# Clustered attention and two mixture layers on one core: a tile for each PSUM bank, weights converted in halves

## The chip, the cores and the metric

The kernel runs on one core of a Trainium2 chip. The metric is the device time of one execution in microseconds (us). The engines are PE (TensorE, matrix multiplies and transposes), ACT (ScalarE), DVE (VectorE), POOL (GpSimd) and SP (SyncE, which here issues nearly all DMAs). Each engine works through its own list of instructions in order and waits on semaphores.

## The reference, cut to what matters

```python
q_assign = argmax(q_n . c_n);  k_assign = argmax(k_n . c_n)      # 16 clusters per head
mask = q_assign[:, :, :, None] == k_assign[:, :, None, :]
scores = where(mask, scale * q @ k.T, -1e9);  attn = softmax(scores)
x = (attn @ v) as 1536 tokens x 512                               # B, H, S, D = 2, 8, 768, 64
h = x @ w_in  (512 x 2048);  x = (h * cos(h)) @ w_out             # first mixture
h = x @ w2_in;  g = h if h >= 1, 0 if h <= -1, else (h + 1)**2 / 4
out = g @ w2_out                                                  # second mixture
```

The weights arrive as 64-bit floating point numbers, two 32-bit words each, and are put together on the chip.

## The kernel before

**Attention** goes through the sixteen heads as eight pairs. A cycle of the program treats one pair and prepares the one two cycles on. What is emitted in a cycle is written out in a string of words (`CYCLE`, with `BEGIN` for the first cycle, `LATE` and `LAST` for the seventh and eighth, and `END` behind them). A quote behind a word means the pair of the cycle before. `S` is a tile of scores (128 rows by 768, four matmuls, L583 and L586) and its row maximum on DVE (L593); `E` its exponential on ACT (L601); `G` three PE transposes of probabilities into one PSUM bank (L644) and their copy to SBUF on ACT (L646); `V` the product with `v` (L651), which adds up in the fourth bank; `T` the other head's transpose on DVE (L677) and `W` its product (L686), which uses all four banks; `X` and `Y` scale and split the first head's result (L656, L663 to L667); `Z` and `z` do so for the second (L696, L697, L705 to L707); `R` and `B` invert the row sums and spread them by DMA. `Q`, `D`, `C`, `m`, `t`, `n`, `O`, `H`, `J`, `L` prepare a pair to come: transposes of q and k (L491), cluster products (L510), their transpose (L518), the first largest (L527 to L538), its transpose (L545, L547), stacking by DMA (`copy`, L473) and loading. `w` is one step of weight conversion.

PSUM has eight banks. Four are held by a single tile, `big`, of four banks; `bank3` hands out its first three in turn to all transposes and cluster products. The scores have two tiles of two banks each. The recording layer that sets the semaphores takes `big` as one thing.

**Weights.** A weight of 512 x 512 comes as two chunks of 128 x 1024 (`issue_chunk`, one raw buffer `wraw`, 1 MB a load), and is converted in six steps (`convert_chunk`): a magnitude on ACT (L157), four integer and clipping steps on DVE (L159 to L167), the high part on POOL (L173), the low part on DVE (L176). Twelve steps, one weight, are done in the last two cycles, the rest between the matmuls of the mixtures.

**Mixtures.** For each of 4 columns of weights and 3 blocks of 512 tokens, `hidden` makes four tiles `h` of 12 matmuls (three products of high and low parts, L859 to L861) in four PSUM banks, and applies the function with ACT and DVE (`g_cosine`: L832 to L838; `g_blend`: L847 to L852), POOL (L821) and DVE (L825) splitting the result. `output` makes four tiles `y` of the block before and adds them up (L905, L914).

What sets the order: `manual_schedule` keeps the order in which the code emits for the attention. It is closed ahead of the mixtures, whose order a scheduler chooses from priorities; it also puts pieces of them among the attention's last instructions.

Of the kernel before, what the change touches and what calls it, by code (L numbers as in the profile page):

```python
# [19 lines left out]
P = 128  # L20
# [6 lines left out]
CHUNK = 6  # L27
P_BUFS = 8
# [5 lines left out]
def attention_moe_moe(  # L34
# [104 lines left out]
    def shared(name):  # L139
        return w0pool.tile([P, 2, 512], F32, tag="wx", bufs=1, name=name)  # L140

    def issue_chunk(n):
        if n >= len(wchunks):
            return
        src, c0, _ = wchunks[n]
        raw = w0pool.tile([P, 2, 512], I64, tag="wraw", bufs=1, name=f"wraw{n}")
        nc.sync.dma_start(raw, src[:, c0:c0 + 2])
        wraw[n] = raw

    def convert_chunk(n):  # L150
# [8 lines left out]
        nc.vector.tensor_scalar(x, x, HIGH_MIN, HIGH_MAX, ALU.max, ALU.min)  # L159
# [12 lines left out]
        hi, lo = t[:, 0, c0:c0 + 2], t[:, 1, c0:c0 + 2]  # L172
        nc.gpsimd.tensor_scalar(hi, x, 1.0, 0.0, ALU.mult, ALU.add)  # L173
        issue_chunk(n + 1)
        yield
        nc.vector.tensor_tensor(lo, x, hi.bitcast(F32), ALU.subtract)  # L176
        yield

    for l, (wi, wo) in enumerate(((w1_in, w1_out), (w2_in, w2_out))):
        for qi in range(NQ):  # L180
            cols = slice(qi * 512, (qi + 1) * 512)
            for s, src in enumerate((wi[:, cols], wo[cols])):
                for c0 in (0, 2):
                    wchunks.append((src.rearrange("(c p) f -> p c f", p=P), c0,
                                    (l * NQ + qi) * 2 + s))
# [16 lines left out]
    def weight(l, qi, s):  # L202
        pump(2 * CHUNK * ((l * NQ + qi) * 2 + s + 1) - at[0])
        t = wslot[((l * NQ + qi) * 2 + s) % len(wslot)]
        return t[:, 0], t[:, 1]


    with ExitStack() as actx:
# [17 lines left out]
        def load_qk(i):  # L226
# [38 lines left out]
        def centroid_setup(ct):  # L265
# [6 lines left out]
            nat[1] = w0pool.tile([P, 2, NJ, 2, D], F32, tag="wraw", bufs=1, name="nat1")  # L272
            nc.scalar.activation(nat[1][:, :, 0, 0, 0:1].rearrange("p s o -> p (s o)"),
# [17 lines left out]
        def first_pair():  # L291

            idle_o = big[:, 3]
# [16 lines left out]
            both = shared("both0")  # L310
            dots = [both[:, 0, :HS].rearrange("p (j s h c) -> p j s h c", s=2, h=2, c=C),
# [64 lines left out]
            dc = both[:, 1, :HS].rearrange("p (j n) -> p j n", n=P)  # L376
# [16 lines left out]
            eqs = both[:, 1, :HS].rearrange("p (h g c) -> p h g c", h=2, c=C)  # L393
# [81 lines left out]
        class Prep:  # L475
# [26 lines left out]
            def dots(self):  # L502
                both = shared(f"both{self.i}")
                self.ohv, self.eq = both[:, 0, :HS], both[:, 1, :HS]
# [144 lines left out]
        def p_v(i, kt):  # L649
            for hf in range(2):  # L650
                nc.tensor.matmul(big[hf * D:(hf + 1) * D, 3, :HS], v_of[i][:, kt],  # L651
                                 pts.pop((i, 2 * kt + hf)), start=kt == 0, stop=kt == NJ - 1)

        def x_rows(i):
            x = rb[2 * i]
            nc.vector.tensor_tensor(x, big[:, 3, :HS], x, ALU.mult)  # L656
# [22 lines left out]
        def p_v_square(i, n, parts):  # L679
            t, vr = sq[i], vr_of[i]  # L680
            for cp in range(12 * n // parts, 12 * (n + 1) // parts):
                for a in range(4):
                    rows = slice(32 * a, 32 * a + 32)
                    for par in range(2):
                        kt, g = divmod(2 * cp + par, 4)
                        nc.tensor.matmul(  # L686
                            big[par * D:(par + 1) * D, a, :NJ * 32],
# [31 lines left out]
        def run_cycle(c, order):  # L719
# [4 lines left out]
            for word in words:  # L724
# [8 lines left out]
                if not 0 <= i < NP and what != "w":  # L733
                    if what == "L" and i == NP:
                        issue_chunk(0)
                    continue
# [50 lines left out]
                elif what == "w":  # L787
                    pump(arg or 1)

        BEGIN = ("L' S3 m' E3 S4 t' S5 E4 H0' n' G0 E5 R0 O' G1 G2 S6 G3 G4 J0' E6 S7 G5 r T6 V0 E7 H1' V1 G6 "  # L790
                 "G7 S8 T7 B0 Q0 J1' E8 G8 G9 Q1 V2 S9 T8 G10 G11 Q2 Q3 L S10 E9 E10 T9 V3 D S11 E11 C m V4 t "
                 "n ")
# [3 lines left out]
        LATE = ("S0 S1 H0' E0 E1 T10' O' V5' S2 S3 E2 w E3 J0' T11' X' G0 S4 E4 w v' S5 W0' W1' R1' J1' E5 R0 "  # L796
                 "w W2' W3' Y' Z' S6 S7 G1 B1' G2 G3 E6 G4 E7 V0 H1' V1 w T6 T7 G5 G6 G7 S8 G8 r G9 G10 E8 w "
                 "S9 B0 T8 V2 E9 V3 S10 G11 w S11 E10 T9 E11 z' V4 ")
        LAST = ("S0 S1 E0 E1 w T10' V5' S2 S3 E2 E3 T11' X' G0 S4 E4 w v' S5 W0' W1' R1' E5 R0 w W2' W3' Y' "
                 "Z' S6 S7 G1 B1' G2 G3 E6 G4 E7 V0 V1 w T6 T7 G5 G6 G7 S8 G8 r G9 G10 E8 w S9 B0 T8 V2 E9 V3 "  # L800
                 "S10 G11 w S11 E10 T9 E11 z' V4 ")
        END = ("T10' V5' T11' X' R1' W0' B1' W1' W2' W3' Z' Y' z' ")
# [4 lines left out]
        manual.close()  # L807
# [55 lines left out]
    def hidden(l, qi, blk):  # L863
# [4 lines left out]
        for f in range(4):  # L868
# [7 lines left out]
            pump(2 if l == qi == blk == 0 else 1)  # L876
        return gh, gl

    def output(l, qi, blk, gh, gl):
        wh, wl = weight(l, qi, 1)  # L880
        for e in range(4):
# [18 lines left out]
            pump(2 if l == qi == 0 else 1)  # L900
# [64 lines left out]
```

## Time and profile before

| | |
|---|---|
| median of three runs | 940.75 us (928.43 to 942.93) |
| the profiled execution | 924.13 us, its span 922.3 us |
| mean granted PE clock | 0.913 |
| busy of the span | PE 808.5, DVE 587.6, ACT 365.1, POOL 254.4 us |

The attention lasts to about 385 us, the mixtures from there to the end. The granted clock is the share of full speed that PE got: 1.0 stands for 2.4 GHz and 0.5 for 1.2 GHz. A busy PE is counted by modelled ends, so its idle time, with what ended it, says more.

### The profile page before, as it was taken

To read this page: it belongs to the slowest core of one execution; us is meant where nothing else is said; L and a number is where in the kernel's file an instruction comes from. 1 tells how busy PE (TensorE), PEld (TensorE's weight loads), DVE (VectorE), ACT (ScalarE), POOL (GpSimd) and SP (SyncE) were. 2 spreads that over 40 slices of the span, in tenths; PEclk is the share of its full clock that TensorE was granted. 3 is DMA by queue.
4 is the path that set the end of the run, shared out by engine and by line. 5 is a ranking of instruction groups with operands and counts; after the bars stand their busy time and mean duration, and the time that the engine had idled before them with its cause. 6 is when DMAs were issued, how large, how long until landed. Compare 5 with 4: busy or idle time off the path is not lost.

```text
span 922.3 us, 12700 instructions
## 1 busy us (share of the span) xinstructions
PE 808.5 (88%) x4957; PEld 619.6 (67%) x4957; DVE 587.6 (64%) x805; ACT 365.1 (40%) x650; POOL 254.4 (28%) x374
## 2 busy tenths in 40 slices
PE   7677777767777777849999999999999999999998
PEld 4445454545454544638888888888888888888887
DVE  4425453653446574688777878888888687764543
ACT  3534353563454454345443344343225433222220
POOL 5123433443242223443222212123332112211110
PEclk8659696997599788979999999999999999999999
DMA  7524635372437422222122212121121221100012
GB/s 172 133 64 93 142 68 140 71 178 72 104 93 173 105 65 53 101 91 91 57 85 90 87 50 92 47 92 45 47 92 47 92 83 54 46 1 1 0 46 92
DMA packets 52621, 74.97 MB, mean 81 GB/s; under 512 B 28977, under 2 KB 36369, under 8 KB 52561
## 3 DMA queue, kind: packets, MB, share of 16 engines
q1 hardware_dynamic: 52272, 73.99, 29.0%
q8 instruction: 39, 0.64, 0.3%
q14 instruction: 22, 0.17, 0.1%
q10 hardware_dynamic: 288, 0.16, 0.1%
HBM read 50.89 MB, written 3.19 MB: 59 GB/s over the span
## 4 chain that ended last, share of the span: by engine, by line
PE 78%; ACT 6%; DVE 6%; issue 4%; DMA 3%; POOL 2%; SPq 1%; ACTq 0%; DVEq 0%; POOLq 0%
PE y L859 9%; PE y L861 9%; PE y L860 9%; PE h L859 9%; PE h L860 9%; PE h L861 9%; PE big L644 6%; PE big L651 4%; PE s L583 3%; PE s L586 3%; PE big L686 3%; ACT p_t L646 3%; DMA st<-tt 2%; DVE nm L593 2%; SPq L473 1%
## 5 line engine op out<-in xcount | busy, mean ns | idle before, releaser
L593 DVE TENSOR_REDUCE nm<-s 128x1 f32<-128x768 f32 x96 | 90.7, 955 | 119.7 <-PE s L586 118.7
L859 PE MATMUL h<-xh,w 128*128 128x512 f32 x384 | 151.2, 394 | 15.1 <-DVE g L838 12.2
L860 PE MATMUL h<-xl,w 128*128 128x512 f32 x384 | 150.7, 393 | 0.0
L861 PE MATMUL h<-xh,w 128*128 128x512 f32 x384 | 150.6, 392 | 0.0
L821 POOL TENSOR_SCALAR gh<-g 128x512 fp32r<-128x512 f32 x96 | 73.4, 765 | 278.8 <-DVE g L852 159.8
L644 PE MATMUL big<-ident,p 128*128 128x128 f32 x288 | 65.2, 347 | 49.7 <-ACT p_t L646 29.3
L601 ACT ACTIVATE p<-s,nm 128x768 f32<-128x768 f32 x96 | 86.3, 899 | 33.9 <-DVE nm L593 31.6
L644 PEld LDWEIGHTS big<-ident,p 128*128 128x128 f32 x288 | 39.2, 171 | 81.8 <-ACT p_t L646 45.0
L859 PEld LDWEIGHTS h<-xh,w 128*128 128x128 f32 x384 | 73.0, 190 | 31.5 <-DVE g L838 12.9
L646 ACT ACTIVATE p_t<-big 128x384 f32<-128x384 f32 x96 | 47.1, 490 | 108.5 <-PE big L644 107.9
L825 DVE TENSOR_TENSOR gl<-g,gh 128x512 fp32r<-128x512 f32 x96 | 74.5, 776 | 21.8 <-POOL gh L821 15.8
L583 PE MATMUL s<-st,st 128*128 128x384 f32 x192 | 82.5, 429 | 3.7 <-ACT p L601 3.4
L848 ACT ACTIVATE p<-h,ones 128x512 f32<-128x512 f32 x48 | 33.0, 688 | 133.0 <-DVE m L847 132.6
L860 PEld LDWEIGHTS h<-xl,w 128*128 128x128 f32 x384 | 73.1, 190 | 15.4 <-issue 0.3
L861 PEld LDWEIGHTS h<-xh,w 128*128 128x128 f32 x384 | 72.8, 190 | 15.3
L157 ACT ACTIVATE wx<-wraw 128x1024 f32<-128x1024 f32 x32 | 36.1, 1129 | 104.9 <-DVE w L176 46.1
L586 PE MATMUL s<-st,st 80*128 80x384 f32 (+1 forms) x192 | 73.6, 383 | 1.9 <-DVE st L429 1.9
L859 PE MATMUL y<-gh,w 128*128 128x512 f32 x192 | 74.7, 389 | 0.0
L860 PE MATMUL y<-gl,w 128*128 128x512 f32 x192 | 74.7, 389 | 0.0
L861 PE MATMUL y<-gh,w 128*128 128x512 f32 x192 | 74.7, 389 | 0.0
L861 PE MATMUL y<-w,gl 128*128 128x512 f32 (+1 forms) x192 | 74.3, 387 | 0.0
L860 PE MATMUL y<-w,gh 128*128 128x512 f32 (+1 forms) x192 | 74.3, 387 | 0.0
(138 smaller groups left out, 1419.5 us busy)
## 6 DMA issues: line engine op xcount, KB each, us to landing
wraw<-in_moe_w_in_dram SPq DMA_DIRECT2D x16, 1024.0 KB
wraw<-in_moe_w_out_dram SPq DMA_DIRECT2D x16, 1024.0 KB
st<-tt SPq DMA_DIRECT2D x63, 192.0 KB
st<-tt SPq DMA_DIRECT2D x16, 384.0 KB
vr<-in_v_dram SPq DMA_DIRECT2D x32, 192.0 KB
nat<-in_q_dram SPq DMA_DIRECT2D x8, 384.0 KB
nat<-in_k_dram SPq DMA_DIRECT2D x8, 384.0 KB
out_dram<-acc SPq DMA_DIRECT2D x11, 256.0 KB
```

The lines of the kernel that those rows point to most:

```text
L583: nc.tensor.matmul(s[:, step, :HS], qt[:, 0, cols], kt[:, 0, kc], start=True, stop=False)
L586: nc.tensor.matmul(s[:, step, :HS], qt[:rows, 1, cols], kt[:rows, 1, kc], start=False, stop=True)
L593: nc.vector.tensor_reduce(nm, s[:, :, :HS], AX.XY, ALU.max, negate=True)
L601: nc.scalar.activation(p.rearrange("p (a n) -> p a n", a=2), s[:, :, :HS], AF.Exp, bias=nm, accum_out=dens[d][:, jj:jj + 1])
L644: nc.tensor.transpose(ps[:, jj * P:(jj + 1) * P], p[:, kt * P:(kt + 1) * P], ident)
L646: nc.scalar.activation(pt, ps, AF.Copy)
L651: nc.tensor.matmul(big[hf * D:(hf + 1) * D, 3, :HS], v_of[i][:, kt], pts.pop((i, 2 * kt + hf)), start=kt == 0, stop=kt == NJ - 1)
L821: nc.gpsimd.tensor_scalar(hi, g, 1.0, 0.0, ALU.mult, ALU.add)
L825: nc.vector.tensor_tensor(lo, g, hi.bitcast(F32), ALU.subtract)
L859: nc.tensor.matmul(o, lh, rh, start=first, stop=False)
L860: nc.tensor.matmul(o, lh, rl, start=False, stop=False)
L861: nc.tensor.matmul(o, ll, rh, start=False, stop=last)
```

## The change

- `big` becomes four tiles of one bank each; `bank3` takes them in turn. `x_sum` (`Z`) has to go bank by bank, four times a copy on ACT and an addition on DVE, where it was one of each.
- A weight comes as four halves of 128 x 512, with two raw buffers and two buffers for the value under way. For the first six halves the clipping and the low part are done on POOL instead of DVE. q and k of a pair get a raw buffer each.
- `BEGIN` has another order: transposes that need few tiles come earlier, `Q0` to `Q3` too, `R0` and `r` later.
- `LATE`, `LAST` and `END` hold 39 steps (6.5 halves) where they held 12 of the old size.
- `manual_schedule` stays open to the end, so the mixtures run in the order in which they are emitted.

```diff
+NPOOL = 6
     def shared(name):
-        return w0pool.tile([P, 2, 512], F32, tag="wx", bufs=1, name=name)
+        return w0pool.tile([P, 512], F32, tag="wx", bufs=2, name=name)
...
-        raw = w0pool.tile([P, 2, 512], I64, tag="wraw", bufs=1, name=f"wraw{n}")
-        nc.sync.dma_start(raw, src[:, c0:c0 + 2])
+        raw = w0pool.tile([P, 512], I64, tag="wraw", bufs=2, name=f"wraw{n}")
+        nc.sync.dma_start(raw, src[:, c])
...
+        side = nc.gpsimd if n < NPOOL else nc.vector
...
-        nc.vector.tensor_scalar(x, x, HIGH_MIN, HIGH_MAX, ALU.max, ALU.min)
+        side.tensor_scalar(x, x, HIGH_MIN, HIGH_MAX, ALU.max, ALU.min)
...
-        issue_chunk(n + 1)
+        issue_chunk(n + 2)
         yield
-        nc.vector.tensor_tensor(lo, x, hi.bitcast(F32), ALU.subtract)
+        side.tensor_tensor(lo, x, hi.bitcast(F32), ALU.subtract)
...
-        big = ps_b.tile([P, 4, 512], F32, name="big")
-        turn_of = [0]
+        big = [ps_b.tile([P, 512], F32, name=f"big{n}") for n in range(4)]
+        turn_of = [2]
         def bank3():
             turn_of[0] += 1
-            return big[:, turn_of[0] % 3, :HS]
+            return big[turn_of[0] % 3][:, :HS]
...
+        def nat_tile(i, s):
+            return w0pool.tile([P, NJ, 2, D], F32, tag="wraw", bufs=2, name=f"nat{i}_{s}")
...
-            o = big[:, :, :NJ * 32].rearrange("p a (j r) -> p a j r", r=32)
-            nc.scalar.activation(xv, o[D:], AF.Copy)
-            nc.vector.tensor_tensor(xv, o[:D], xv, ALU.add)
+            for a in range(4):
+                o = big[a][:, :NJ * 32].rearrange("p (j r) -> p j r", r=32)
+                nc.scalar.activation(xv[:, a], o[D:], AF.Copy)
+                nc.vector.tensor_tensor(xv[:, a], o[:D], xv[:, a], ALU.add)
...
-        BEGIN = ("L' S3 m' E3 S4 t' S5 E4 H0' n' G0 E5 R0 O' G1 G2 S6 G3 G4 J0' E6 S7 G5 r T6 V0 E7 H1' V1 G6 "
-                 "G7 S8 T7 B0 Q0 J1' E8 G8 G9 Q1 V2 S9 T8 G10 G11 Q2 Q3 L S10 E9 E10 T9 V3 D S11 E11 C m V4 t "
+        BEGIN = ("L' S3 G0 m' E3 t' G2 S4 G4 E4 n' S5 H0' E5 Q0 O' G1 Q1 G3 S6 V0 Q2 Q3 L J0' E6 G5 G6 S7 T6 V1 E7 G7 H1' G8 S8 T7 E8 G9 G10 S9 V2 T8 J1' E9 R0 r G11 D S10 V3 E10 T9 C m B0 S11 E11 V4 t n ")
...
-        LAST = ("S0 S1 E0 E1 w T10' V5' S2 S3 E2 E3 T11' X' G0 S4 E4 w v' S5 W0' W1' R1' E5 R0 w W2' W3' Y' "
+        LAST = ("S0 S1 E0 w w E1 T10' V5' S2 w S3 E2 w E3 w T11' X' w G0 S4 E4 w w v' S5 W0' W1' R1' E5 R0 w w W2' W3' Y' Z' S6 S7 G1 B1' G2 G3 E6 G4 E7 w V0 V1 w T6 T7 w G5 G6 G7 S8 G8 r G9 G10 E8 w w S9 B0 T8 V2 w E9 V3 S10 G11 w S11 E10 T9 w E11 z' V4  ")
-        END = ("T10' V5' T11' X' R1' W0' B1' W1' W2' W3' Z' Y' z' ")
+        END = ("T10' V5' T11' w w X' R1' W0' B1' W1' w w W2' W3' Z' w w Y' z' ")
...
-        manual.close()
         flush()
...
-            pump(2 if l == qi == blk == 0 else 1)
+            pump(2)
...
-            pump(2 if l == qi == 0 else 1)
+            pump(4 if l == qi == 0 else 2)
```

On PE, in the third cycle behind `W`, before the change: the last matmul of `S7`, then two of three transposes each of `G1`, `G2` and `G3` and the first of `C`, all into `big` (the brackets name the engine whose semaphore is waited for).

```order
L586 MATMUL s31_1271<-st1_2_1_498,st0_2_1_497 128x384
L644 MATMUL big_87<-ident_60,p27_1088 128x128 [waits DVE_49]
L644 MATMUL big_87<-ident_60,p28_1115 128x128
L644 MATMUL big_87<-ident_60,p24_1027 128x128 [waits Activation_49]
L644 MATMUL big_87<-ident_60,p25_1042 128x128
L644 MATMUL big_87<-ident_60,p27_1088 128x128 [waits Activation_49]
L644 MATMUL big_87<-ident_60,p28_1115 128x128
L518 MATMUL big_87<-ident_60,both4_1097 128x128 [waits Activation_49]
```

Each bank's first transpose waits for an engine, and by the program's semaphores that is the one that read `big` last, whichever bank it read. The same place after the change:

```order
L589 MATMUL s31_1296<-st1_2_1_414,st0_2_1_413 128x384
L647 MATMUL big1_88<-ident_60,p27_1105 128x128 [waits DVE_49]
L647 MATMUL big1_88<-ident_60,p28_1133 128x128
L647 MATMUL big2_89<-ident_60,p24_1044 128x128 [waits DVE_49]
L647 MATMUL big2_89<-ident_60,p25_1059 128x128
L647 MATMUL big0_87<-ident_60,p27_1105 128x128
L647 MATMUL big0_87<-ident_60,p28_1133 128x128
L521 MATMUL big1_88<-ident_60,eq4_1115 128x128 [waits Activation_49]
L647 MATMUL big2_89<-ident_60,p24_1044 128x128 [waits Activation_49]
```

The order is the same and the banks have names of their own; `G1` and `G2` still wait for DVE, for its reading of their own bank in `Z`, and `G3` does not wait; `C` and `G4` wait for the copies of `G1` and `G2`, three turns back.

On DVE, where attention ends and the mixtures begin, before: `wx` is a weight chunk under way, `xs` the last head's sum, `r` and `g` the function of the first tile `h`.

```order
L176 TENSOR_TENSOR w_3474<-wx_3580,w_3474 128x1024 [waits Pool_49]
L697 TENSOR_TENSOR xs_3449<-big,xs_3449 64x4x6x32 [waits Activation_49]
L833 SCALAR_TENSOR_TENSOR r_0_0_0_3496<-n_0_0_0_3495,h_0_0_0_3482 128x512 [waits DMAHW4_49,DMAHW3_49,DMAHW5_49,DMAHW1_49,Activation_49]
L159 TENSOR_SCALAR wx_3700<-wx_3700 128x1024 [waits Activation_49]
L161 TENSOR_SCALAR wx_3700<-wx_3700 128x1024 [waits DVE_49]
L164 SCALAR_TENSOR_TENSOR wx_3700<-wraw_3658,wx_3700 128x1024 [waits DMAHW4_49,DVE_49]
L833 SCALAR_TENSOR_TENSOR r_0_0_1_3521<-n_0_0_1_3520,h_0_0_1_3507 128x512 [waits Activation_49]
L838 SCALAR_TENSOR_TENSOR g_0_0_0_3497<-r_0_0_0_3496,h_0_0_0_3482 128x512 [waits Activation_49]
L167 SCALAR_TENSOR_TENSOR wx_3700<-wraw_3658,wx_3700 128x1024 [waits DVE_49]
```

After the change, from the last two pieces of `xs` on:

```order
L701 TENSOR_TENSOR xs_3554<-big_89,xs_3554 64x6x32 [waits Activation_49]
L701 TENSOR_TENSOR xs_3554<-big_90,xs_3554 64x6x32 [waits Activation_49]
L161 TENSOR_SCALAR wx_3504<-wx_3504 128x512
L163 TENSOR_SCALAR wx_3504<-wx_3504 128x512 [waits DVE_49]
L831 SCALAR_TENSOR_TENSOR r_0_0_0_3607<-n_0_0_0_3606,h_0_0_0_3593 128x512 [waits DMAHW5_49,DMAHW2_49,DMAHW6_49,DMAHW1_49,DMAHW7_49,DMAHW0_49,Activation_49]
L166 SCALAR_TENSOR_TENSOR wx_3504<-wraw_3379,wx_3504 128x512 [waits DMAHW2_49,DVE_49]
L169 SCALAR_TENSOR_TENSOR wx_3504<-wraw_3379,wx_3504 128x512 [waits DVE_49]
L836 SCALAR_TENSOR_TENSOR g_0_0_0_3608<-r_0_0_0_3607,h_0_0_0_3593 128x512 [waits Activation_49]
L831 SCALAR_TENSOR_TENSOR r_0_0_1_3634<-n_0_0_1_3633,h_0_0_1_3620 128x512 [waits Activation_49]
```

Ahead of the first `r` there stand two steps on a half of conversion where a whole chunk and more stood, and between the first `r` and its `g` stand two steps on a half where a chunk's first three steps and the second tile's `r` stood.

## Rows read from the trace of the kernel before

**Rows 1.** Busy time by stretch (us; x instructions): attention's cycles, their sum, mixtures.

```profile
20.00:88.00 68.00, 47.34 (x203) 30.15 (x203) 29.32 (x41) 30.34 (x63) 16.38 (x24) 0.70 0.41 98
88.10:132.20 44.10, 33.29 (x327) 21.55 (x326) 21.19 (x31) 20.67 (x43) 16.59 (x25) 0.81 0.47 108
176.60:218.80 42.20, 31.36 (x335) 21.33 (x342) 21.61 (x32) 20.89 (x44) 16.57 (x25) 0.91 0.48 113
345.00:379.60 34.60, 26.48 (x285) 17.30 (x284) 21.98 (x32) 14.61 (x29) 11.22 (x18) 0.81 0.22 66
sum 359.46, PE 265.55 PEld 174.81 DVE 183.97 ACT 166.63 POOL 115.17; mean PE 33.19 PEld 21.85 DVE 23.00 ACT 20.83 POOL 14.40
...
500.00:600.00 100.00, 100.00 (x443) 82.84 (x442) 79.56 (x108) 40.50 (x64) 19.41 (x25) 1.00 0.22 73
```

**Rows 2.** What PE waited for: us in all, times, longest.

```profile
PE big L644 <- ACT p_t L646: 29.3, 49, 0.6
PE big L644 <- DVE rb L656: 16.2, 7, 2.5
PE h L859 <- DVE g L838: 12.2, 1, 12.2
PE big L651 <- DVE both L528: 8.4, 6, 1.8
PE big L651 <- ACT oht L547: 7.1, 6, 2.4
PE big L651 <- ACT p_t L646: 4.8, 8, 0.7
PE big L491 <- ACT t L497: 3.7, 7, 0.7
PE big L545 <- ACT t L497: 3.7, 5, 0.8
```

**Rows 3.** Timeline, third cycle: start, length, instructions [idle before <- releaser].

```profile
129.22 0.48 ACT L512 ACTIVATE both<-big 128x384 f32<-128x384 f32 x1
129.74 0.56 DVE L656 TENSOR_TENSOR rb<-big,rb 128x384 f32<-128x384 f32 x1 [0.55 <-ACT both L512]
130.35 0.55 PE L644 MATMUL big<-ident,p 128*128 128x128 f32 x3 [2.25 <-DVE rb L656]
...
139.00 0.49 ACT L646 ACTIVATE p_t<-big 128x384 f32<-128x384 f32 x1 [1.63 <-PE big L644]
...
139.54 0.55 PE L644 MATMUL big<-ident,p 128*128 128x128 f32 x3 [0.58 <-ACT p_t L646]
```

**Rows 4.** Timeline from the last `W` to PE's next matmul.

```profile
379.60 4.59 PE L686 MATMUL big<-ptb,vr 32*64 32x192 f32 x192
...
393.43 1.04 POOL L173 TENSOR_SCALAR w<-wx 128x1024 fp32r<-128x1024 f32 x1 [6.47 <-DVE wx L167]
...
398.60 1.13 ACT L157 ACTIVATE wx<-wraw 128x1024 f32<-128x1024 f32 x1 [7.77 <-DMA wraw<-in_moe_w_in_dram]
...
404.52 0.68 DVE L838 SCALAR_TENSOR_TENSOR g<-r,h 128x512 f32<-128x512 f32 x1
...
405.25 0.80 PE L859 MATMUL h<-xh,w 128*128 128x512 f32 x1 [12.22 <-DVE g L838]
```

**Rows 5.** Groups of instructions by line: busy us, mean ns, idle before.

```profile
L696 ACT ACTIVATE xs<-big 64x768 f32<-64x768 f32 x8 | 6.5, 807 | 18.9 <-PE big L686 18.8
L838 DVE SCALAR_TENSOR_TENSOR g<-r,h 128x512 f32<-128x512 f32 x48 | 32.6, 680 | 4.3 <-ACT r L835 4.3
L832 ACT ACTIVATE n<-h 128x512 int32<-128x512 f32 x48 | 28.0, 584 | 22.7 <-PE h L861 22.7
L834 ACT ACTIVATE r<-r 128x512 f32<-128x512 f32 x48 | 30.4, 632 | 63.5 <-DVE r L833 63.3
L825 DVE TENSOR_TENSOR gl<-g,gh 128x512 fp32r<-128x512 f32 x96 | 74.5, 776 | 21.8 <-POOL gh L821 15.8
```

**Rows 6.** Line 176 alone: ns least, median, longest.

```profile
L176 DVE TENSOR_TENSOR w<-wx,w x32: 1209/1224/2296, 329.9 to 807.5; 128x1024 fp32r<-128x1024 f32 x32
```

More of the change, by code (lines that the diff above doesn't have):

```diff
@@ L182, in attention_moe_moe @@
             for s, src in enumerate((wi[:, cols], wo[cols])):
-                for c0 in (0, 2):
-                    wchunks.append((src.rearrange("(c p) f -> p c f", p=P), c0,
+                for c in range(4):
+                    wchunks.append((src.rearrange("(c p) f -> p c f", p=P), c,
                                     (l * NQ + qi) * 2 + s))
@@ L229, in load_qk @@
                 t = ap.tile([P, 2, NJ, 2, D], F32, tag="ptb", bufs=1, name="nat0")
-            elif i == 1:
-                t = nat[1]
+                t = [t[:, 0], t[:, 1]]
             else:
-                t = w0pool.tile([P, 2, NJ, 2, D], F32, tag="wraw", bufs=1, name=f"nat{i}")
+                t = nat[1] if i == 1 else [nat_tile(i, s) for s in range(2)]
             for s, src in enumerate((q, k)):
                 nc.sync.dma_start(
-                    t[:, s], src[b, 2 * hp:2 * hp + 2].rearrange("h (p j) d -> p j h d", j=NJ))
+                    t[s], src[b, 2 * hp:2 * hp + 2].rearrange("h (p j) d -> p j h d", j=NJ))
             nat[i] = t
+        def nat_tile(i, s):
+            return w0pool.tile([P, NJ, 2, D], F32, tag="wraw", bufs=2, name=f"nat{i}_{s}")
         def load_v(i):
@@ L271, in centroid_setup @@
             sq = nc.scalar.activation(y, ss[:, 0:1], AF.Sqrt)
-            nat[1] = w0pool.tile([P, 2, NJ, 2, D], F32, tag="wraw", bufs=1, name="nat1")
-            nc.scalar.activation(nat[1][:, :, 0, 0, 0:1].rearrange("p s o -> p (s o)"),
+            nat[1] = [nat_tile(1, s) for s in range(2)]
+            nc.scalar.activation(nat[1][0][:, 0, 0, 0:2],
                                  desc[:, 0:2], AF.Exp, scale=0.0)
@@ L291, in first_pair @@
         def first_pair():
-            idle_o = big[:, 3]
+            idle_o = big[3]
             def run_idle(n):
@@ L502, in dots @@
             def dots(self):
-                both = shared(f"both{self.i}")
-                self.ohv, self.eq = both[:, 0, :HS], both[:, 1, :HS]
+                self.ohv, self.eq = (shared(f"{n}{self.i}")[:, :HS] for n in ("ohv", "eq"))
                 cw = cn32[:, self.hp].rearrange("p h c -> p (h c)")
@@ L650, in p_v @@
             for hf in range(2):
-                nc.tensor.matmul(big[hf * D:(hf + 1) * D, 3, :HS], v_of[i][:, kt],
+                nc.tensor.matmul(big[3][hf * D:(hf + 1) * D, :HS], v_of[i][:, kt],
                                  pts.pop((i, 2 * kt + hf)), start=kt == 0, stop=kt == NJ - 1)
@@ L655, in x_rows @@
             x = rb[2 * i]
-            nc.vector.tensor_tensor(x, big[:, 3, :HS], x, ALU.mult)
+            nc.vector.tensor_tensor(x, big[3][:, :HS], x, ALU.mult)
         def x_parts(i):
@@ L686, in p_v_square @@
                         nc.tensor.matmul(
[L687 removed]
+                            big[a][par * D:(par + 1) * D, :NJ * 32],
                             vr[rows, g, kt * D:(kt + 1) * D],
```

32 lines of the change are left out of this document (14 added, 18 removed).

## The prediction

> **What bounds the kernel now.** I read the busy time by stretch first [rows 1]. In the mixtures PE is busy 100 of 100 us at full clock: 443 matmuls in 100 us, 0.226 us each, and all 2304 of them (2 layers x 4 columns x 3 blocks x 8 tiles x 12) take 520 us whatever else happens. DVE, the next busiest, is at 80% there. So the mixtures can lose time, and gain none. The other 400 us are another matter. From 20 to 379.6 us PE is busy 265.6 of 359.5 us, DVE 184.0, ACT 166.6: no engine is full, so engines wait for each other. Second come PE's waits [rows 2]. Nearly everything that PE waits for in attention stands in front of a write to `big`. The seven rows on `big` sum to 29.3 + 16.2 + 8.4 + 7.1 + 4.8 + 3.7 + 3.7 = 73.2 us, of the 93.9 us that PE idles in that stretch.
>
> Third comes the timeline, which tells what kind of waits these are [rows 3]. A transpose group starts at 139.54, the moment the copy that began at 139.00 and took 0.49 ends, although that copy reads another bank: transposes and copies alternate where three banks could overlap them. And DVE's L656, which reads the fourth bank, starts at 129.74 just as ACT's L512, which reads one of the first three, has ended (129.22 + 0.48); PE's next transposes wait 2.25 us until L656 is through. Every access is ordered against the last access of another engine to any part of `big`. That is an order that the program asks for, no matter of data.
>
> Last I looked at the junction [rows 4]. The last `W` ends at 379.60 + 4.59 = 384.2; PE then does the rest of the first four tiles `h`, and idles 12.22 us until the function of the first one frees its bank. In between DVE and ACT, in the scheduler's order, stand behind a weight chunk: POOL's high part at 393.43, then ACT's L157 at 398.60, which waited 7.77 us for a load into the only raw buffer.
>
> **The change part by part.** *Own tiles for the banks.* The waits of 73.2 us lose their ground; what stays are true ones: a transpose on the copy three turns back, a product on the copies that it reads, `W` on `X`. In the cycle from 176.6 to 218.8 [rows 1] PE was busy 31.4 of 42.2 us at clock 0.91, that is 28.6 us of work at full clock, where ACT has 20.9 and DVE 21.6. PE would be the bound by a wide margin, but the engines run in order, and a score tile waits for a row maximum on DVE and an exponential on ACT before its buffer is free, so some waits come back. I take 62 us of the 73.2 as gained (nearer to the whole, since after the change a copy of 0.49 us has two more transpose groups of 0.55 us to hide behind [rows 3]). Bounds: 33, if more than half returns as waits on ACT and DVE, and 80, if small waits left out above go too.
>
> *The clock.* The granted clock is 0.70 on the mean of the first stretch, 0.81 from 88.1 to 132.2 and 0.91 from 176.6 to 218.8; in the mixtures, where PE never idles, it is 1.00 [rows 1]. The difference between 0.81 and 0.91 is 33.3 - 31.4 = 1.9 us of PE a cycle [rows 1]. A denser PE should be nearer to the best cycle; over the seven cycles behind the first I take 7 x 1.9 = 13, bounds 0 and 44 (at full clock 33.3 us at 0.81 become 27.0, 6.3 less a cycle).
>
> *`x_sum` in four.* ACT's copy took 0.81 us for 768 columns [rows 5]; a piece of 192 costs between 0.2 (a quarter) and 0.49 (the row for 384 columns, [rows 3]). That is 0 to 1.2 us more on ACT a cycle, and as much on DVE, both behind `W` where PE has two score tiles to do. I count 0.3 a cycle, 2.5 in all, bounds 0 and 9.
>
> *The new first cycle.* PE idles 20.7 of 68 us there at clock 0.70 [rows 1]; most of that is in the term above. For the order itself I take 2 us, bounds -2 (a load that now comes later is waited for) and 8.
>
> *More steps ahead, and the mixtures in emitted order: the junction.* After the last `W` the list of DVE has four short pieces of `x_sum`, two steps on a half, `r`, two steps on a half, `g`. With an estimate of 0.4 for each of the eight short ones (half to two thirds of the 0.68 of L838, [rows 5]), 0.68 each for `r` and `g`, and ACT's n, sine and square (0.58, 0.63 and another 0.63) behind a table load, the first `g` stands some 7 us behind `W`. PE has 48 matmuls x 0.226 = 10.8 us to do before it needs that bank. So the wait of 12.22 us goes [rows 4]; next late are the splits of the last head's result on POOL, some 7 to 8 us behind `W`, still ahead of the second block at 10.8. I take 11, bounds 4 and 14. Steps that move into the last cycles stand on ACT, POOL and DVE among the score tiles. DVE has 22.0 of 34.6 us of work there [rows 1] and gives its clipping and low parts to POOL, which has 11.2. I count nothing for them, bound 8.
>
> The Trainium skill, SBUF — State Buffer, section Who interferes with whom, says that a DVE instruction with two SBUF inputs and a POOL instruction that reads SBUF take turns on one port, each blocked for the other's whole length. The row for L176 fits it: 1.224 us in the median and 2.296 at the longest [rows 6]. By that rule the eighteen POOL steps of the first six halves would hold DVE up; this is a rival below, worked out from the row.
>
> *Halves in the mixtures.* Five DVE steps of 128 x 512 cost about 0.68 each [rows 5], so two of them 0.14 more than one L176 of 1.224 [rows 6]: 5 x 32 x 0.14 = 22 us more of DVE over some 520 us, from 80% to 84%. PE hides it. If that cover were gone it would be up to 22.
>
> *Mixtures in emitted order.* PE's order of matmuls stays the same. In a `hidden` step the list runs n, r, sine, square, g, low part: 0.58 + 0.68 + 0.63 + 0.63 + 0.68 + 0.78 = 3.98 us [rows 5] where PE needs 12 x 0.226 = 2.71. Four steps lag 4 x 1.27 = 5.1 us if nothing overlaps; the four steps of `output` behind them give 10.8 us to make it up, and four banks stand between. I take 0, bounds 0 and 10.
>
> **The sum.** 62 + 13 - 2.5 + 2 + 11 = 85.5 us off a span of 922.3: 836.8, and with the 1.8 us between span and execution 838.6. The median of the runs is 940.75 / 924.13 = 1.018 times the profiled execution; so 854, say 852.
>
> **The rivals.** *The waits return.* ACT and DVE in order, or a slow clock, take over what `big` gives up: the gain is 33 + 0 - 2.5 + 11 = 41.5, that is 882.6 and 898 in the median. For it speaks that each score tile goes through three engines with two buffers, against it that ACT and DVE are under 55% busy.
>
> *PE runs dense.* Each cycle behind the first comes to 30 us: PE work of 28.6 and little else. From 88.1 to 379.6 are 291.5 us, which become 210; the first stretch gives 18 of its 20.7 idle us and the junction 12: 111 us, 811 to 813 for the execution, 828 in the median. The alternation in rows 3 speaks for it, the in-order lists against.
>
> *POOL's conversion holds up DVE.* Eighteen steps x (2.296 - 1.224) = 19 us, if each comes at a bad moment on the path: 858, in the median 873. Against it stands that DVE idles a third of the last cycles.
>
> *The mixtures stall: slower.* If in emitted order the lag of `hidden` is not made up, each of 96 steps shows 1.27 us: 122 us. 838.6 + 122 = 961, median 978. It decides where a step's chain, conversions included, passes 2 x 2.71 = 5.4 us; its parts sum to 4.0, and two conversion steps, five of six on DVE at 0.68, bring it to 5.1. So there is room, not much.
>
> *It does not do what it says.* If the recording layer still ordered the four tiles as one, only the junction would gain: 927. The program's waits after the change name single banks, so I give it 1 in 100.
>
> **How the numbers follow.** Forecast 0.54; waits return 0.17; dense 0.17; POOL 0.07; mixtures stall 0.04; no effect 0.01. The range from 812 to 900 takes in the dense case at its low side and the returning waits at the high side. Within 2% is about what a measurement can tell from no change: that is above 922. A gain this small needs waits below the lower bound, or part of the stall: 0.04 the same, 0.03 slower, 0.93 faster.
>
> **What would show it.** In the profile after: PE's waits on ACT's p_t copies and on L656 gone or below 15 us in all; cycles from `W` to `W` of 33 to 36 us where those of rows 1 took 42 and 44; a granted clock above 0.85 in attention; no wait of 12 us behind the last `W`; PE at 100% in the mixtures with 0.226 us a matmul. I am wrong if the cycles stay above 40 us (then the score tiles' chain or the DMAs were the bound), or if PE idles inside the mixtures.

## The result, and the profile after

The changed kernel takes 780.93 us in the median of four runs (780.18 to 782.06), the kernel before 936.62 in the same comparison: a ratio of 0.836, 95% interval 0.829 to 0.843. The direction was right, the size was not: 852 with a range from 812 to 900 was forecast. The profiled execution took 782.06 us, its span is 780.1.

The table splits the spans of the two profiled executions at the first and at the last `W` (busy time is PE's, from the windows).

| stretch | before: us, PE busy | after: us, PE busy | shorter by |
|---|---|---|---|
| start to first `W` | 88.0, 62.9 | 53.1, 46.7 | 34.9 |
| to the last `W` | 291.5, 218.3 | 194.7, 175.4 | 96.8 |
| the last `W` | 4.6, 4.6 | 6.4, 6.4 | -1.8 |
| behind it, mixtures | 538.1, 522.7 | 525.9, 522.7 | 12.2 |

Attention is 130.0 us shorter. PE idles 72.7 us less in it, and its busy time, for the same matmuls, falls by another 57.3 us. The windows of the kernel after show it, the first two lines for the first two rows of the table, the others cycle by cycle; the second fence has the first two rows for the kernel before. A line gives the window, its length, the busy time of PE, PEld (PE's loading of weights), DVE, ACT and POOL with their instructions, the granted clock, the busy share of the DMA engines and GB/s, as in [rows 1].

```profile
0.00:53.10 53.10, 46.70 (x265) 30.39 (x266) 36.48 (x71) 36.04 (x77) 28.01 (x73) 0.97 0.82 190
53.10:247.80 194.70, 175.41 (x2196) 129.54 (x2195) 153.48 (x238) 132.49 (x303) 117.98 (x166) 0.95 0.66 160
...
20.00:53.10 33.10, 29.09 (x168) 19.37 (x168) 24.13 (x34) 23.69 (x53) 14.91 (x23) 0.95 0.80 183
53.10:78.50 25.40, 25.40 (x327) 19.16 (x326) 21.22 (x34) 20.00 (x46) 16.59 (x25) 1.00 0.82 194
104.60:132.60 28.00, 26.05 (x328) 19.33 (x327) 22.64 (x34) 19.96 (x46) 16.77 (x25) 1.00 0.73 175
184.50:218.30 33.80, 26.25 (x307) 19.54 (x306) 25.23 (x39) 19.17 (x43) 21.32 (x25) 0.90 0.51 129
218.30:247.80 29.50, 22.02 (x286) 15.16 (x285) 20.62 (x34) 14.75 (x34) 17.58 (x23) 0.79 0.30 84
350.00:450.00 100.00, 100.00 (x443) 82.79 (x442) 81.98 (x137) 40.19 (x67) 22.79 (x31) 1.00 0.22 67
```

```profile
0.00:88.00 88.00, 62.88 (x266) 38.25 (x266) 36.49 (x71) 37.95 (x77) 27.94 (x73) 0.73 0.51 121
88.10:379.60 291.50, 218.25 (x2195) 144.67 (x2194) 154.68 (x214) 136.30 (x278) 98.80 (x152) 0.83 0.43 104
```

The five cycles behind the first, 40 to 47 us before, take 25.4 to 28.0, at full clock and with hardly an idle moment of PE. Only the last two cycles, in which weights are converted, are long and slow, 33.8 and 29.5 us. The mixtures run as before, 443 matmuls in 100 us. PE's waits, all that are left in attention above 1.5 us in sum (us in all, times, longest):

```profile
PE s L586 <- ACT p L604: 7.8, 9, 4.1
PE big L647 <- ACT p L604: 4.6, 4, 2.5
PE big L647 <- DVE xs L701: 4.4, 1, 4.4
PE big L689 <- DVE rb L659: 1.6, 1, 1.6
PE big L689 <- DVE ptb L680: 1.6, 1, 1.6
```

The waits on ACT's copies, 29.3 us in [rows 2], are gone. At the junction there is no wait on `g` either, and PE waits for nothing in the mixtures. The timeline of the last cycle but one shows where the 4.4 us come from:

```profile
191.14 1.01 POOL L617 TENSOR_SCALAR line<-turned 6x32 f32<-6x32 f32 x4 [1.97 <-DMA flat<-line]
192.23 1.91 POOL L161 TENSOR_SCALAR wx<-wx 128x512 f32<-128x512 f32 x1
194.18 0.43 DVE L163 TENSOR_SCALAR wx<-wx 128x512 int32<-128x512 int32 x1 [4.57 <-POOL wx L161]
194.64 1.15 DVE L701 TENSOR_TENSOR xs<-big,xs 64x192 f32<-64x192 f32 x4
195.05 2.18 PE L647 MATMUL big<-ident,p 128*128 128x128 f32 x9 [4.36 <-DVE xs L701]
```

POOL clips a half (L161) behind work that waits for a DMA; DVE's next step on that half (L163) waits 4.57 us for it, `x_sum` stands behind L163 in DVE's list, and PE's transposes wait for `x_sum`.

### The profile page after: what moved, and what is told of

The parts are those of the page before. It is cut to its first block, busy times and chain, and to the rows that moved or that the text cites. A ratio compares the mean times of both kernels' runs of the same rounds, so it can differ in the third digit from the quotient of the medians.

```text
span 780.1 us, 13106 instructions
## 1 busy us (share of the span) xinstructions
PE 751.2 (96%) x4956; PEld 598.4 (77%) x4957; DVE 602.3 (77%) x977; ACT 364.3 (47%) x706; POOL 280.2 (36%) x418
## 4 chain that ended last, share of the span: by engine, by line
PE 89%; DVE 6%; issue 2%; POOL 2%; ACT 1%; DMA 0%; POOLq 0%; ACTq 0%; DVEq 0%
PE h L857 11%; PE h L858 11%; PE h L859 11%; PE y L857 11%; PE y L858 11%; PE y L859 11%; PE s L586 4%; PE big L647 4%; PE big L689 4%; PE big L654 3%; PE s L589 3%; DVE nm L596 2%; PE big L495 1%; DVE ptb L680 1%; POOL wx L161 1%
## 5 line engine op out<-in xcount | busy, mean ns | idle before, releaser
L819 POOL TENSOR_SCALAR gh<-g 128x512 fp32r<-128x512 f32 x96 | 64.8, 675 | 221.4 <-DVE g L850 131.5
L175 POOL TENSOR_SCALAR w<-wx 128x512 fp32r<-128x512 f32 x64 | 52.2, 815 | 157.4 <-DVE wx L169 153.5
L604 ACT ACTIVATE p<-s,nm 128x768 f32<-128x768 f32 x96 | 86.9, 905 | 32.3 <-DVE nm L596 29.6
L857 PEld LDWEIGHTS h<-xh,w 128*128 128x128 f32 x384 | 72.1, 188 | 15.2 <-issue 0.3
L859 PEld LDWEIGHTS h<-xh,w 128*128 128x128 f32 x384 | 72.1, 188 | 15.0
L586 PE MATMUL s<-st,st 128*128 128x384 f32 x192 | 75.0, 391 | 8.5 <-ACT p L604 7.8
L858 PE MATMUL y<-w,gh 128*128 128x512 f32 (+1 forms) x192 | 74.3, 387 | 0.0
L857 PE MATMUL y<-w,gh 128*128 128x512 f32 (+1 forms) x192 | 74.3, 387 | 0.0
L823 DVE TENSOR_TENSOR gl<-g,gh 128x512 fp32r<-128x512 f32 x96 | 65.6, 683 | 6.8 <-POOL gh L819 6.0
L912 DVE TENSOR_TENSOR acc<-y,acc 128x512 f32<-128x512 f32 x71 | 48.5, 684 | 25.5 <-PE y L859 25.3
L589 PE MATMUL s<-st,st 80*128 80x384 f32 (+1 forms) x192 | 66.5, 346 | 0.0
L586 PEld LDWEIGHTS s<-st,st 128*128 128x128 f32 x192 | 37.7, 196 | 25.8 <-ACT p L604 20.0
```

The costliest lines, as they stand in the source:

```text
L586: nc.tensor.matmul(s[:, step, :HS], qt[:, 0, cols], kt[:, 0, kc], start=True, stop=False)
L589: nc.tensor.matmul(s[:, step, :HS], qt[:rows, 1, cols], kt[:rows, 1, kc], start=False, stop=True)
L604: nc.scalar.activation(p.rearrange("p (a n) -> p a n", a=2), s[:, :, :HS], AF.Exp, bias=nm, accum_out=dens[d][:, jj:jj + 1])
L819: nc.gpsimd.tensor_scalar(hi, g, 1.0, 0.0, ALU.mult, ALU.add)
L823: nc.vector.tensor_tensor(lo, g, hi.bitcast(F32), ALU.subtract)
L857: nc.tensor.matmul(o, lh, rh, start=first, stop=False)
```

## The experiments

My theory after the result: the four tiles alone bring the attention's gain, half as waits that go and half as PE work that then runs at full clock. The rivals: the other parts (the first cycle, conversions, POOL) bring a good share; or the clock has nothing to do with it. The kernels were measured in five comparisons, in each of which the kernel before ran beside them, with medians from 931.3 to 936.6 us; so a difference of one or two us between kernels of different comparisons is not read.

| kernel | median us | range | ratio to before, interval |
|---|---|---|---|
| e1_tiles_only | 781.43 | 780.96 to 783.24 | 0.839, 0.833 to 0.845 |
| e2_one_tile | 944.45 | 938.71 to 955.84 | 1.012, 1.002 to 1.022 |
| e3_old_begin | 783.63 | 781.66 to 784.72 | 0.842, 0.835 to 0.849 |
| e4_sched | 789.37 | 788.59 to 792.21 | 0.848, 0.842 to 0.854 |
| e5_npool0 | 771.05 | 768.69 to 772.88 | 0.826, 0.821 to 0.831 |
| e6_fourth_bank | 872.46 | 867.33 to 874.94 | 0.934, 0.927 to 0.940 |
| e7_few_steps | 797.93 | 795.28 to 799.49 | 0.854, 0.848 to 0.860 |
| e8_double_scores | 973.07 | one run | none |
| e9_low_on_pool | 769.98 | 768.53 to 774.18 | 0.829, 0.821 to 0.837 |
| e10_few_late | 771.40 | 769.59 to 771.73 | 0.830, 0.824 to 0.837 |
| e11_low_few | 772.07 | 770.26 to 773.09 | 0.831, 0.825 to 0.838 |
| e12_tiles_emitted | 777.56 | 776.53 to 781.61 | 0.834, 0.828 to 0.840 |

### The tiles alone, and all but the tiles

e1 is the kernel before with the lines of the change on `big`, `bank3` and `x_sum`, and nothing else. e2 is the changed kernel with

```diff
-        big = [ps_b.tile([P, 512], F32, name=f"big{n}") for n in range(4)]
+        whole = ps_b.tile([P, 4, 512], F32, name="big")
+        big = [whole[:, n] for n in range(4)]
```

> The kernel before with nothing changed but the four tiles in place of `big` (and with them x_sum in four pieces). In the changed kernel the attention is 130.0 us shorter: 34.9 in the first cycle, 96.8 in the seven others, 1.8 lost in the last W; the junction brings another 12.2. Theory, the tiles do it: PE's idle time in attention goes (about 73 us) and the granted clock follows (about another 59 us less of busy time for the same work), so the seven cycles shorten by 85 to 97 us, the first by 20 to 30, and the junction keeps its 12 us wait: execution 797 to 820, ratio 0.86 to 0.88, granted clock in attention 0.92 or more. Rival, the tiles remove only the waits and the clock stays near 0.83, the rest coming from the other parts: 845 to 865, ratio 0.92.

> The changed kernel with its four banks as slices of one tile again (the layer then orders all accesses to them as one); everything else stays as changed. Theory, the tiles carry the attention's gain: 97 us come back in the cycles and some 20 in the first one, the junction's 12 stay: 885 to 905, waits on ACT's copies back to some 30 us, granted clock in attention back to 0.85 or less. Rival, the first cycle, the raw buffers and the conversions carry a good part: 815 to 850.

e1 measured 781.43, as fast as the whole change and faster than its theory: the seven cycles take 179.0 us where 291.5 were before, 112.5 less and not 85 to 97. Its windows: a dense cycle, the last two, and the stretch from the last `W` to the first wait's end; under them PE's wait there.

```profile
56.10:81.50 25.40, 25.40 (x327) 19.15 (x326) 21.24 (x34) 20.02 (x46) 16.62 (x25) 1.00 0.74 180
185.50:214.00 28.50, 25.96 (x307) 18.99 (x306) 22.83 (x33) 17.90 (x41) 11.58 (x17) 0.88 0.52 139
214.00:235.10 21.10, 19.29 (x282) 14.21 (x281) 19.29 (x31) 14.15 (x32) 12.48 (x17) 1.00 0.36 108
235.10:262.50 27.40, 13.99 (x234) 11.35 (x233) 17.43 (x25) 7.40 (x13) 13.20 (x14) 0.84 0.25 85
```

```profile
PE h L860 <- DVE g L839: 13.4, 1, 13.4
```

The same dense cycles, so the tiles are the cause. The last `W` ends at 235.11 + 4.63 = 239.7, where the changed kernel's ends at 254.2, 14.5 us later. Its last two cycles and last `W` take 69.7 us where e1's take 54.2, so what the change adds there costs 15.5; its five cycles ahead of them lose 2.0, and its first cycle is 3.0 shorter. The junction still has its wait, 13.4 us, and the part behind the last `W` takes 540.1 us for 525.9: 14.2 that the change gains there. The two cancel, so all the other parts together are worth nothing on top of the tiles.

e2 measured 944.45, beyond both expectations: all that the tiles gave is gone, and by its ratio it is no faster than the kernel before, if not slightly slower. Its first cycle behind the first `W` and its waits:

```profile
83.00:130.80 47.80, 35.86 (x327) 23.73 (x326) 22.12 (x34) 21.27 (x47) 16.62 (x25) 0.75 0.42 100
```

```profile
PE big L648 <- ACT p_t L650: 29.7, 47, 2.0
PE big L648 <- DVE rb L660: 17.9, 7, 3.4
PE big L648 <- DVE xs L702: 14.4, 7, 5.3
```

The waits of [rows 2] are back, with 14.4 us on `x_sum`, whose four pieces now alternate between ACT and DVE on one tile. The clock is back at 0.75 with them. So the tiles are shown from both sides: alone they bring the whole gain, and without them the other parts bring none, here with the pieces of `x_sum` against them.

### The first cycle's order, and the mixtures' order

e3 puts the old `BEGIN` string into the changed kernel. e4 puts `manual.close()` back ahead of `flush()`.

> The changed kernel with the old order of the first cycle (BEGIN); everything else stays. The first stretch went from 88.0 us to 53.1. Theory, most of it is the tiles' doing and the order itself is worth the 2 us that I predicted: 780 to 787. Rival, the new order is what shortens it: the first stretch comes to 65 us or more, 793 to 815 in all.

> The changed kernel with manual_schedule closed ahead of the mixtures, as before, so that the scheduler orders them and may put pieces of them among the attention's last instructions. Theory, the junction's 12.2 us come from the emitted order (the first g no longer stands behind conversions): 789 to 796, with a wait of 8 to 12 us of PE for the first g. Rival, they come from the finished weight and the shorter steps, whatever the order: 779 to 784, no such wait.

e3: 783.63, 2.7 us more than the changed kernel and within its theory, but little more than runs of one kernel differ by (781.66 to 784.72 here); the first `W` starts at 54.96 where it started at 53.13. e4: 789.37, 8.4 us slower. The finished weight is there as in the changed kernel, and the wait returns all the same, as this line of its waits shows: with the halves and the finished weight, the scheduler's order brings it back. That the order alone does not take it away is shown by e12 below.

```profile
PE h L858 <- DVE g L837: 11.2, 1, 11.2
```

### POOL's share of the conversion

e5 sets `NPOOL = 0`. e9 leaves the low part on POOL and clips on DVE:

```diff
-        side.tensor_scalar(x, x, HIGH_MIN, HIGH_MAX, ALU.max, ALU.min)
+        nc.vector.tensor_scalar(x, x, HIGH_MIN, HIGH_MAX, ALU.max, ALU.min)
```

> The changed kernel with NPOOL = 0: the clipping and the low part of the first six halves are done on DVE again, everything else stays. The tiles alone gave 781.4 with a last W that ends at 239.7 us, where the changed kernel's ends at 254.2: the steps that it puts in the last cycles cost some 14 us, as much as its junction gains. Theory, it is POOL: its clipping takes 1.91 us a half (DVE's 0.42), DVE waits 11.5 us for it in three places, PE stands behind DVE's x_sum and the score tiles for 12 us more, and the clock falls after it: without POOL 764 to 773. Rival, it is the number of steps, whoever does them (DVE gets 18 instructions, 6.7 us more, and is the fullest engine of the last two cycles): 778 to 790.

> The changed kernel, of whose first six halves only the low part is done on POOL and the clipping on DVE. Without any of it on POOL the time was 771.05. Theory, it is the clipping that hurts (DVE's next step waits for it, in a queue of POOL that stands behind other work), the low part ends a chain that nothing on DVE waits for: 767 to 772. Rival, POOL's low part hurts by itself (1.27 us where DVE takes 0.69, ahead of the splits that PE needs): 774 to 781.

e5: 771.05, e9: 769.98, both some 10 us faster than the changed kernel and equal to each other, as the theories said; in e5 the last `W` ends at 244.2 where it ended at 254.2. (Twelve instructions move to DVE in e5, not the 18 of its expectation; their 6.7 us are right.) So the clipping is what hurts, and the low part on POOL costs nothing that can be measured. L161 in the kernel after (ns least, median, longest): the form on POOL takes 1.91 us, on DVE 0.42, and DVE waited for POOL's 11.5 us in three places.

```profile
L161 DVE TENSOR_SCALAR wx<-wx x58: 412/420/569, 255.7 to 688.1; 128x512 f32<-128x512 f32 x58
L161 POOL TENSOR_SCALAR wx<-wx x6: 1913/1914/1915, 179.8 to 239.4; 128x512 f32<-128x512 f32 x6
...
  DVE wx L163: 11.5, 3
```

### Fewer steps in the last cycles

e7 takes NPOOL = 0, `LATE` and `LAST` of before with each `w` doubled, the old `END`, and `pump(3 if l == qi == 0 and blk < 2 else 2)` in `hidden`. e10 takes NPOOL = 0 and four steps less: `END` begins `T10' V5' T11' X'`, `LAST` ends `S10 G11 S11 E10 T9 E11 z' V4`. e11 is e10 with the low part on POOL.

> The changed kernel with NPOOL = 0 and only 24 half steps in the last two cycles (two where the kernel before had one), none in END, and three steps in place of two behind each tile of the first two hidden blocks. Theory, the last cycles lose because they are given more than DVE can do beside the score tiles: last W ends near 240 us, PE dense behind it, 764 to 770. Rival, the work left for the first hidden blocks holds up their functions there: a wait of PE of 5 us or more in the first 30 us of the mixtures, 772 to 785.

> The changed kernel with NPOOL = 0 and without four of its 39 steps: the two ahead of X in END and the last two in LAST (they move behind the mixtures' first tiles). In the run with NPOOL = 0 PE waited 2.55 us for the last transposes on DVE and 1.20 for X, and the last W then ran at half clock, 7.1 us for 4.16. Theory, DVE's steps right ahead of the last transposes and X cause this: last W 4.2 to 5 us long and ended by 240, 764 to 768. Rival, the steps only move and PE waits for them in the first blocks: 769 to 775.

> Both together: only the low part on POOL, and four steps fewer ahead of the mixtures. If both theories hold: 761 to 767, the fastest so far; if the low part on POOL hurts by itself, 770 or more.

All three theories fall, and e10 comes out where its rival said. e10's last `W` is dense again and ends at 239.6, as its theory said, 4.6 us ahead of e5's, but 771.40 and 772.07 are no better than e5: behind the last `W` e10 takes 529.7 us where e5 takes 525.9. PE is busy 53.19 of 55.80 us there, waiting for `g` and for weights that come later. The window is from 244.20 on, the waits from 184 us to the end of e10.

```profile
244.20:300.00 55.80, 53.19 (x231) 42.73 (x231) 46.42 (x74) 28.61 (x50) 21.24 (x26) 1.00 0.24 73
```

```profile
PE h L857 <- DVE g L836: 1.0, 2, 0.8
PE y L857 <- POOL w L175: 1.0, 1, 1.0
PE y L859 <- DVE w L178: 0.6, 1, 0.6
```

e7, 797.93, loses in two places that neither side had named. Behind its last `W` it takes 546.5 us where e5 takes 525.9: its weight for `output` is late, the first row below, while the functions that the rival named cost PE 2.9 us. And its last cycle but one takes 33.8 us where e5's takes 28.0: two steps in a row put DVE's low part right behind POOL's high part, DVE waits there, and `x_sum` and PE's transposes behind it, the other rows (the timeline of e7).

```profile
PE y L861 <- POOL w L175: 10.4, 2, 7.5
```

```profile
191.85 0.97 DVE L178 TENSOR_TENSOR w<-wx,w 128x512 fp32r<-128x512 f32 x1 [2.28 <-POOL w L175]
192.85 1.15 DVE L701 TENSOR_TENSOR xs<-big,xs 64x192 f32<-64x192 f32 x4
...
193.26 1.92 PE L647 MATMUL big<-ident,p 128*128 128x128 f32 x12 [3.16 <-DVE xs L701]
```

### What the clock follows

e6 gives the fourth bank a tile of its own and leaves the other three one tile (`x_sum` in two pieces). e8 computes every score tile of the kernel before twice, to the same values:

```diff
-        big = ps_b.tile([P, 4, 512], F32, name="big")
+        three = ps_b.tile([P, 3, 512], F32, name="big")
+        big = [three[:, n] for n in range(3)] + [ps_b.tile([P, 512], F32, name="big3")]
```

```diff
+            for _ in range(2):
+                nc.tensor.matmul(s[:, step, :HS], qt[:, 0, cols], kt[:, 0, kc],
+                                 start=True, stop=False)
+                nc.tensor.matmul(s[:, step, :HS], qt[:rows, 1, cols], kt[:rows, 1, kc],
+                                 start=False, stop=True)
```

> The kernel before with the fourth bank a tile of its own and the other three still one tile (x_sum in two pieces). It takes away the waits on rb, on the maximum and on the one-hots (16.2 + 8.4 + 7.1 + 4.8 us, of up to 2.5 us each) and leaves those of the transposes on ACT's copies (29.3 us, 49 of 0.6 us). Theory, the clock goes down with the longer waits: it comes back here to 0.95 or more in attention, and with it most of the 59 us: 835 to 855. Rival, the many short waits hold it down as well: clock 0.85 to 0.90, 865 to 890.

> The kernel before, one tile, with the four matmuls of every score tile done twice (the same values are written again): 768 matmuls more, 48 a half cycle, 96 a whole one... that is 12 tiles x 0.72 us = 8.6 us of PE at full clock in each cycle. PE's waits on the tile stay as they are. Theory, a denser PE gets a better clock, which pays for part of the work: granted clock in attention 0.90 or more, cycles 46 to 49 us where they took 42 to 44, 955 to 975. Rival, the clock has nothing to do with how dense PE is, 8.6 us become 10.4 at a clock of 0.83: cycles of 53 to 54 us, 1000 to 1012.

The count of matmuls in e8's expectation is wrong: they are 384 more, 48 a cycle; the 8.6 us are right. e6 measured 872.46: by its time the rival's side, by its clock between the two. Its cycles, two of seven, and their sum:

```profile
76.70:115.20 38.50, 31.29 (x327) 21.17 (x326) 21.69 (x32) 20.85 (x45) 16.59 (x25) 0.87 0.54 124
115.20:150.50 35.30, 27.57 (x331) 18.90 (x330) 21.78 (x31) 20.71 (x44) 16.58 (x25) 0.99 0.58 135
76.70:325.50 248.80, 198.06 (x2192) 132.95 (x2191) 153.59 (x219) 136.62 (x285) 100.05 (x151) 0.91 0.50 121
```

The second row is worth most. It has the waits on ACT's copies (29.6 us in the whole run, 3.6 in this cycle), at a clock of 0.99. PE's busy time there is 27.57 us; before it was 33.29 in a like cycle at 0.81 [rows 1], and 25.40 in the dense cycle of the kernel after. So 5.7 us of a cycle are the clock. The other 2.2 us I put down to the ends of groups that stand alone, an estimate: three transposes alone take 0.55 us [rows 3], nine in a chain 1.15 in the kernel after, 0.17 a lone group, and PE waits twelve times in this cycle.

e8: 973.07, one run. Six cycles took 302.6 us where 256.9 were before, 7.6 more each, at a clock of 0.85 for 0.83 and with the same waits. First the kernel before, then e8:

```profile
88.10:345.00 256.90, 191.77 (x1915) 127.37 (x1914) 132.71 (x183) 121.69 (x250) 87.58 (x134) 0.83 0.45 109
```

```profile
92.40:395.00 302.60, 243.50 (x2199) 188.03 (x2198) 132.04 (x182) 123.50 (x251) 87.81 (x134) 0.85 0.39 92
```

Neither expectation holds: the time is one that the theory allowed, its clock and its cycles are not. PE's busy time in the same cycles grew by 243.5 - 191.8 = 51.7 us, as much as 6 x 8.6 us cost at full clock. By tiles, the score matmuls take 137.4 us for 76.1, which is 61.2 more, and those into `big` 124.6 for 131.3. So the added work ran partly below full clock and the rest gained a little, some 10 us of 61 in all. Work added beside the waits bought little of the clock; taking the waits away did (e1, and in part e6). Which of the waits brings it down is not settled. In e6 the cycles from 76.70 and from 115.20 have the same waits of PE, row by row, within 0.1 us, but for one of 0.4, at clocks of 0.87 and 0.99; and three transposes behind a wait of 0.58 us take 0.90 us in the one, at a granted clock of 0.51, and 0.55 in the other, at 1.00.

```profile
84.92 0.90 PE L645 MATMUL big<-ident,p 128*128 128x128 f32 x3 [0.58 <-ACT p_t L647]
...
123.72 0.55 PE L645 MATMUL big<-ident,p 128*128 128x128 f32 x3 [0.58 <-ACT p_t L647]
```

### Two parts alone

e12 is e1 without `manual.close()`: the tiles and the emitted order, nothing else.

> The kernel before with two parts of the change alone: the four tiles, and the mixtures in emitted order (manual_schedule not closed ahead of them). Weights stay in whole chunks with one raw buffer, BEGIN, LATE, LAST and END stay old. The tiles alone gave 781.43, with a PE wait of 13.4 us at the junction. Theory, the emitted order removes that wait here as well and the other parts are not needed: 766 to 772. Rival, the only raw buffer needs the scheduler: in emitted order ACT stands in its list behind a load (7.8 us in the junction before), the functions of the tiles wait behind it, and PE idles inside the mixtures: 785 or more, with waits on g all along.

777.56, between the two. The wait of 13.4 us goes, but waits of 3.3 + 2.9 + 0.4 = 6.6 us at the start of the mixtures take its place (below, the waits of e12).

```profile
PE h L859 <- DVE g L838: 3.3, 2, 1.8
...
PE y L859 <- POOL w L173: 2.9, 1, 2.9
...
PE y L861 <- DVE w L176: 0.4, 1, 0.4
```

The rival's mechanism falls: behind these PE never waits in the mixtures, with one raw buffer and ACT's list in emitted order. But only a part of the junction's loss is gone. These are the ends of the last `W` in e12 and in e4:

```profile
235.74 1.19 PE L686 MATMUL big<-ptb,vr 32*64 32x192 f32 x36 [0.27 <-issue]
```

```profile
248.86 4.12 PE L689 MATMUL big<-ptb,vr 32*64 32x192 f32 x180 [0.41 <-DVE rb L659]
```

From there to the end of their spans (774.7 and 790.4) e12 takes 537.8 us and e4 537.4, where e1 takes 540.1 and the changed kernel 525.9. In e1 and e4 the scheduler has put 8 and 12 matmuls of the mixtures ahead of that, 0.23 us each. With these counted, e1 loses 16.0 us against the changed kernel, e4 14.2, and e12 11.9, of which 6.6 are the waits and 5.2 more busy time of PE, whose clock is 0.90 from 250 to 300 us. So the emitted order alone takes away 4 of the 16 us, the halves and the finished weight alone 2, and both together all: the junction's gain needs both.

## Why the prediction was wrong

**The step that failed is the clock.** It said "A denser PE should be nearer to the best cycle; over the seven cycles behind the first I take 7 x 1.9 = 13", and measured are 57.3 us less of PE's busy time in attention, 42.8 of them in those seven cycles. Three things were wrong in it. The best cycle of the kernel before, at 0.91, was no ceiling: it had waits as the others have, and in the kernel after, without them, the clock is 1.00 in the five cycles behind the first. The first cycle, at 0.70, was left out; it alone gave 16.2 us. And the ends of lone groups, by the estimate above 2.2 us a cycle, had no term. The upper bound of 44 was right for the seven cycles, and the value was taken near the lower one. That short idle times can do this is in the Trainium skill, TensorE: Matmul & The Clock Gate, section A second HAM failure mode: psum-queue depth-cycling: short idle times of PE between groups that cycle through banks made the clock swing between its two levels. The rows agree: a product of four matmuls of the same form in one cycle of the kernel before, the first time at half clock (1.2 GHz, granted 0.50), the second at full (2.4 GHz, granted 1.00).

```profile
146.13 1.55 PE L651 MATMUL big<-p_t,v 128*64 128x384 f32 x4 [1.33 <-DVE both L528]
...
162.35 0.87 PE L651 MATMUL big<-p_t,v 128*64 128x384 f32 x4
```

**The floor of 28.6 us** under the rival of a dense PE came from 31.4 us times 0.91. That counts the ends of groups that stand alone as work, by the estimate above 2.2 of the 3.2 us; PE's cycle in the kernel after takes 25.4. So even the dense rival, 828, was too slow, though its mechanism is the one that happened.

**The waits.** Of the 73.2 us that the term started from, 1.3 lay ahead of the stretch that it named, which changes little. 62 us were taken, less 0.5 for `x_sum` and the first cycle's order; 72.7 us of idle time went, and 81.0 by the tiles alone: to the end of the last `W` PE idled 384.1 - 285.7 = 98.4 us before, and 239.7 - 222.3 = 17.4 in e1. The mechanism was right and the gain near its upper bound of 80. Few waits came back on ACT and DVE: in the five cycles behind the first PE is busy 127.1 of 131.4 us.

**The steps in the last cycles** were counted as nothing, bound 8; they cost 15.5 us with the last `W`. POOL is about 10 of it (e5, e9), by DVE's wait for POOL's clipping. The rival on POOL named the right place and the wrong way: it argued from instructions that block each other. Such blocking is in the trace: L166 took 1.42 us at 210.29, while POOL's L711 ran from 209.35 to 211.16, where L166 takes 0.69 in the median. The Trainium skill, SBUF — State Buffer, section Who interferes with whom, agrees with that row. But of the eighteen steps that the rival counted, six, the high parts, were on POOL before the change too, and e9, which leaves six more there, the low parts, loses nothing by them: that is not where the time went.

**The junction:** 11 predicted, 12.2 measured between the two profiles, and 8.4 us of time lost in e4. Right, and for the reason given, the emitted order with shorter steps: alone, the order takes away 4 us of 16 and the steps 2 (e12, e4). **The mixtures** neither stalled nor gained: no wait of PE there. Halves on DVE cost nothing that shows.

**The factor from span to median.** I multiplied by 1.018, because the kernel before ran that much longer in the median than in its profile, and took 852 for the 854 that came out. The changed kernel's median is its profile's time, 780.93 for 782.06. In sum: 44.3 us of the miss are PE's busy time, that is the clock and the ends of lone groups, 11.2 the idle time, 1.2 the junction, and 14.4 this factor: 71.1 us from 852 to 780.9.

## What to carry to other kernels

Where an engine's busy time and its clock are both below full, price the removal of waits twice: the idle time, and the busy time that the granted clock and the ends of lone groups add; the second was 57 us here, the first 73. A buffer that the layer orders as one thing should be one tile for each part that is used on its own. A step handed to a slower engine should not stand in the middle of a chain that comes back: here its end could be handed over, as the low part, but not its start, as the clipping. Changes that cancel, like the last cycles and the junction here, show only when each is run alone, and parts that need each other, like the two of the junction, only when both are left out in turn. The fastest kernels here, at 770 to 772 us, are the changed one with the clipping on DVE.

## What the hardware showed unexpectedly

POOL took 1.91 us for a maximum and minimum over 128 x 512 (L161), twice its own 0.96 in the median for a multiply and add of that size (L175, 0.62 at the least), and 4.6 times DVE's 0.42. And the kernel with the waits varies more from run to run: the kernel before from 928.79 to 942.00, 1.4%, in the seven runs beside e12, the kernels with four tiles by 0.2 to 0.7% in four runs each; whether the clock's swings make that was not tried.
